# ACT squares q and k, the softmax is issued two heads ahead, and v is split at the turn

## The chip, the cores and the metric

One core of a Trainium2 chip runs the whole program. The metric is the device time of one execution in microseconds (us). TensorE is called PE, VectorE DVE, ScalarE ACT, GpSimd POOL; SP is the queue from which nearly all transfers are issued.

## What is computed

The reference is an attention with a root-mean-square norm on q and k, and two mixers behind it:

```python
batch, n_heads, seq, head_dim = (4, 12, 448, 64)
q_n, k_n = (rmsnorm(q, g_q), rmsnorm(k, g_k))     # x / sqrt(mean(x*x) + 1e-6) * g
scores = scale * np.matmul(q_n, k_n.transpose(0, 1, 3, 2))
scores = scores - np.max(scores, axis=-1, keepdims=True)
attn = np.exp(scores)
attn = attn / (np.sum(attn, axis=-1, keepdims=True) + 1e-09)
out = np.matmul(attn, v)
# mixer 1: u = x + (U V applied over tokens);  y = u + relu(u @ w_ch1) @ w_ch2   (768 -> 3072 -> 768)
# mixer 2: u = x + (w_tok1, relu, w_tok2 over tokens); out = u + relu(u @ w_ch1) @ w_ch2   (768 -> 1536 -> 768)
```

There are 4 x 12 = 48 heads of 448 tokens by 64 values, all in float32.

## The kernel before

The program works in stages. In the first, the **lone stage**, PE has nothing but attention: the 24 heads of the first two batches (12 pairs of heads). Then the mixers of these two batches run, with the attention of the other 24 heads spread among their matmuls; the loop that does this takes one step of `attention` for so many matmul steps of the mixer (`run`). The last stages are mixers alone. `attention` is a generator: one step `t` of it issues one head's product and another head's softmax. The step at which the lone stage ends is called the seam (`seam` = 24).

For a pair of heads the work is this, with its lines:

- `fetch_heads` (L359) loads q, k and v of the pair, 112 partitions by 512 values each. q and k share 5 buffers (tag `qkr`), v has 3.
- `load_pair` squares q and k into `sq` (L373, one buffer), sums the squares on DVE into `ms` (L374), makes 1/sqrt of the mean by Ln and Exp on ACT and a Newton step (L376 to L384), and multiplies it in to give `qn` and `kn` (L392). Squares and these multiplications are one function `mul`: DVE for pairs 0, 2 and 3, POOL for all others. Behind that, still in `load_pair`, v is split into a high and a low part `vs` (L144 on ACT, L145 on POOL), except the even head of a lone-stage pair, which is multiplied whole.
- `turn_pair` transposes `qn` and `kn` on PE (L410), splits them into high and low halves `both` (L417 and L421 on ACT, L418 and L422 on DVE), and sends them through eight transfers on the SP queue into the tiles `qs` and `ks` of the two heads (L433, L434; three buffers each).
- `softmax` makes the scores of a head in four chunks of 112 rows: two matmuls into a bank `sc` (L79; three banks in the lone stage), the row maximum on DVE (`nm`, L451), the exponential with its sum on ACT (`p`, L453), and for each two chunks the reciprocal of the sums (L456, L457) and the scaling of `p` on POOL (L460). `p` has 12 tiles in the lone stage, three heads.
- `weigh` is the product with v: for each of four column blocks PE transposes the four `p` tiles (`pt`, L479), ACT copies the result to `ph` (L490), DVE takes the rest `pl` (L494; for whole heads there is no `pl`, and DVE copies every second `ph`, L488), and PE multiplies them with v into `pv` (L79). The result goes to `xT` by DVE (L499, or ACT's `tmp` L502 and DVE's L503).

In step `t`, softmax of head `t+1` and product of head `t` are issued by turns, then `turn_pair` of the pair of head `t+3`, `fetch_heads` of head `t+7`'s, `load_pair` of head `t+5`'s, where those are even. That is the order in which the program is written. A scheduler then sorts the instructions of each engine within the limits of tiles and banks; the order in which an engine executes is what it decided, and each engine takes its instructions strictly in that order.

Right behind the seam the first weights of the mixer are converted (`to_f32`: load `w_raw` L116, ACT L125 and L130, DVE L126, L127, L131, POOL L134; split L144, L145), and `rank_mix` transposes `xT` (L552) as its first step.

Of the kernel before, what the change touches and what calls it, by code (L numbers as in the profile page):

```python
# [9 lines left out]
F32 = mybir.dt.float32  # L10
# [3 lines left out]
AF = mybir.ActivationFunctionType  # L14
# [10 lines left out]
def attention_then_two_mixers(  # L25
# [30 lines left out]
    nc = tc.nc  # L56
# [43 lines left out]
    pools = {"late": False, "split_u": nc.gpsimd}  # L100
    AT = dict(qr=5, kr=5, vr=3, qn=1, vs=2, p=8, ph=3, pl=3, sq=1)

# [260 lines left out]

    def load_pair(b, hp, whole, turn, qk):
        first = turn == 0
        mul = nc.vector.tensor_mul if turn in (0, 2, 3) else nc.gpsimd.tensor_mul
        qr, kr, vr = qk + fetch_heads(b, hp, "v")

        ms = pools["at"].tile([CP, 2, 8], F32, tag="ms", name="ms")
        for i, t in enumerate((qr, kr)):  # L370
            sq = pools["at"].tile([CP, 2 * NC4, D], F32, tag="sq", bufs=AT["sq"], name="sq")
            tt = t.rearrange("p h c d -> p (h c) d")
            mul(sq, tt, tt)  # L373
            nc.vector.reduce_sum(ms[:, i], sq, axis=AX.X)  # L374
# [4 lines left out]
        nc.scalar.activation(rs, rs, AF.Exp, scale=-0.5)  # L379
        nt = pools["at"].tile([CP, 2, 8], F32, tag="nt", name="nt")  # L380
        small.tensor_mul(nt, rs, rs)
# [12 lines left out]
        qn, kn = qn[0], kn[0]  # L394

        vs = pools["at"].tile([CP, 2, NC4, 2, D], F32R, tag="vs", bufs=AT["vs"], name="vs")
        js = [j for j in range(2) if j not in whole]
# [3 lines left out]
        flat = vr.rearrange("p h c d -> p (h c d)")  # L401
        return qn, kn, [flat[:, j * NC4 * D:] if j in whole else vs[:, j] for j in range(2)]

# [101 lines left out]
    def attention(pairs, seam):  # L505

        n = 2 * len(pairs)
        loaded, turned, probs, fetched = {}, {}, {}, {}  # L510
        dst = None

        def soft(h):
            if not 0 <= h < n:
                return iter(())
            probs[h] = []
            return softmax(probs[h], *turned[h // 2][h % 2])

        for t in range(-7, n):
            if t == seam:  # L520
                for _ in soft(t):
                    pass
            steps = [soft(t + 1) if t + 1 != seam else iter(())]
            if t >= 0:
                if t % 2 == 0:
                    dst = pairs[t // 2][3]()
                steps.append(weigh(
                    probs.pop(t), loaded[t // 2][2][t % 2], t % 2, dst, t % 2 in pairs[t // 2][2]))
# [7 lines left out]
            h = t + 7  # L536
            if h < n and h % 2 == 0:
                fetched[h // 2] = fetch_heads(*pairs[h // 2][:2], "qk")
            h = t + 5
            if 0 <= h < n and h % 2 == 0:  # L540
                loaded[h // 2] = load_pair(
                    *pairs[h // 2][:3], h // 2, fetched.pop(h // 2))
                if h == 0:
                    turned[0] = turn_pair(*loaded[0][:2], first=True)
            yield t

# [491 lines left out]
    with ExitStack() as stack:  # L1038
# [128 lines left out]
```

## Time and profile before

| | us |
|---|---|
| median of 3 runs | 1530.44 (1529.71 to 1535.4) |
| the profiled execution's own time | 1532.7 |
| its span, first to last instruction | 1530.9 |
| PE busy in the span | 1440.5 (94%) |
| DVE busy | 1170.5 (76%) |
| POOL busy | 921.8 (60%) |
| ACT busy | 742.7 (49%) |

The profiled execution is 2.3 us above the median of the runs, and its span 1.8 us below its own time. Busy time of PE is the time in which a matmul is somewhere in its pipeline, so it overstates how full the engine is. These shares are means over all stages; the change touches the attention, and most of it the lone stage, the first 201 us or so.

### The profile page before, as it was taken

What the parts mean: (1) busy time and instruction counts of PE and PEld (TensorE: products, weight loads), DVE (VectorE), ACT (ScalarE), POOL (GpSimd) and SP (SyncE); (2) the same over time, 40 slices, a digit from 0 to 9 for tenths busy, and PEclk for the clock granted to TensorE, in tenths of its full rate; (3) what the DMA queues carried; (4) which work ended last, traced back from release to release, by engine and by line L of the source; (5) the groups of instructions that cost most, each with busy time, mean ns of one, the idle gap of its engine ahead of it and who ended that gap; (6) DMA issues with size and microseconds to landing.
All of it is one profiled execution on the core that took longest, in us unless ns stands there. A gap on an engine that the chain in (4) does not pass through costs nothing.

```text
span 1530.9 us, 22094 instructions
## 1 busy us (share of the span) xinstructions
PE 1440.5 (94%) x7396; PEld 1271.6 (83%) x7396; DVE 1170.5 (76%) x1793; ACT 742.7 (49%) x1508; POOL 921.8 (60%) x955
## 2 busy tenths in 40 slices
PE   4889978999999999999999999998999999999998
PEld 3667656888899889988888998897999998988997
DVE  7888777887877778666757766477888888578876
ACT  4777655656665665444535343335343431334421
POOL 5899857877876655455645454037777755206841
PEclk9999979999999999999999999999999999999999
DMA  6666545867766664765637664354545453424343
GB/s 171 159 163 162 145 162 183 250 193 218 253 220 203 184 208 171 258 227 175 214 128 240 227 231 143 116 194 134 177 127 183 127 186 129 134 85 127 119 122 103
DMA packets 144385, 266.06 MB, mean 174 GB/s; under 512 B 12832, under 2 KB 104448, under 8 KB 144160
## 3 DMA queue, kind: packets, MB, share of 16 engines
q1 hardware_dynamic: 143952, 264.65, 55.5%
q8 instruction: 59, 0.97, 0.3%
q14 instruction: 54, 0.44, 0.1%
q10 hardware_dynamic: 320, 0.00, 0.0%
HBM read 149.72 MB, written 79.10 MB: 149 GB/s over the span
## 4 chain that ended last, share of the span: by engine, by line
PE 63%; DVE 11%; POOL 8%; DMA 7%; ACT 5%; issue 4%; SPq 1%; ACTq 0%; POOLq 0%; DVEq 0%
PE ps_x L79 26%; PE ps_g L79 12%; PE ps_p L79 10%; PE pv L79 3%; PE sc L79 3%; PE pt L479 2%; POOL w_bits L134 2%; PE ps_u L79 2%; POOL w L145 2%; PE ps_t L79 2%; DMA qs<-both 2%; DVE w_bits L126 1%; POOL p L460 1%; DMA w_raw<-in_moe_w_ch_dram 1%; DMA c_a<-w_bits 1%
## 5 line engine op out<-in xcount | busy, mean ns | idle before, releaser
L79 PE MATMUL ps_x<-gs,w 128*128 128x448 f32 x1440 | 323.9, 371 | 9.6 <-DVE xT L668 5.3
L79 PE MATMUL ps_g<-u,w 128*128 128x448 f32 x1440 | 313.1, 370 | 4.3 <-DMA w<-h_a 1.8
L79 PEld LDWEIGHTS ps_x<-gs,w 128*128 128x128 f32 x1440 | 266.7, 189 | 35.4 <-DVE xT L668 8.4
L79 PEld LDWEIGHTS ps_g<-u,w 128*128 128x128 f32 x1440 | 269.4, 189 | 28.8 <-DVE u L565 2.1
L79 PE MATMUL ps_x<-gs,w_b 128*128 128x448 f32 x1026 | 228.8, 369 | 7.1 <-DVE xT L833 2.4
L79 PEld LDWEIGHTS ps_x<-gs,w_b 128*128 128x128 f32 x1026 | 192.9, 189 | 25.9 <-DVE xT L833 3.8
L134 POOL TENSOR_TENSOR w_bits<-w_bits,w_round 128x768 uint32<-128x768 uint32 (+3 forms) x80 | 144.9, 1812 | 109.3 <-DVE w_bits L131 59.5
L145 POOL TENSOR_TENSOR w<-w_bits,w 128x768 fp32r<-128x768 f32 (+3 forms) x82 | 145.4, 1780 | 73.1 <-ACT w L144 69.3
L668 DVE TENSOR_TENSOR xT<-ps_x,xT 128x448 f32<-128x448 f32 x216 | 132.2, 617 | 36.5 <-PE ps_x L79 33.7
L145 POOL TENSOR_TENSOR w_b<-w_f,w_b 128x384 fp32r<-128x384 f32 x104 | 118.3, 1152 | 59.1 <-ACT w_b L144 58.9
L295 POOL TENSOR_TENSOR w_f<-w_f 128x384 f32<-128x384 f32 x26 | 36.2, 1391 | 179.8 <-DMA w_f<-c_b 75.0
L460 POOL TENSOR_SCALAR p<-p,sm 112x448 f32<-112x448 f32 x192 | 133.1, 706 | 17.5 <-DVE sm L457 10.9
L453 ACT ACTIVATE p<-sc,nm 112x448 f32<-112x448 f32 x192 | 121.3, 635 | 45.8 <-DVE nm L451 40.3
L79 PE MATMUL sc<-ks,qs 128*112 128x448 f32 x384 | 120.9, 407 | 15.9 <-ACT p L453 11.3
L451 DVE TENSOR_REDUCE nm<-sc 112x1 f32<-112x448 f32 x192 | 116.2, 614 | 17.6 <-PE sc L79 16.8
L479 PEld LDWEIGHTS pt<-ident,p 112*112 112x112 f32 x768 | 89.8, 134 | 33.2 <-issue 10.4
L126 DVE TENSOR_SCALAR w_bits<-w_bits 128x768 f32<-128x768 f32 (+3 forms) x80 | 71.9, 898 | 56.6 <-ACT w_bits L125 56.5
L479 PE MATMUL pt<-ident,p 112*112 112x112 f32 x768 | 111.9, 261 | 2.5 <-DVE pl L494 0.8
L130 ACT ACTIVATE w_round<-w_raw 128x768 uint32<-128x768 uint32 (+3 forms) x80 | 69.8, 873 | 77.6 <-POOL w_bits L134 69.9
L490 ACT ACTIVATE ph<-pt 112x448 fp32r<-112x448 f32 (+1 forms) x168 | 88.2, 544 | 26.2 <-PE pt L479 25.5
L637 ACT ACTIVATE gs<-ps_g 128x448 fp32r<-128x448 f32 x88 | 47.3, 541 | 108.8 <-PE ps_g L79 107.9
L125 ACT ACTIVATE w_bits<-w_raw 128x768 f32<-128x768 f32 (+3 forms) x80 | 69.8, 874 | 61.7 <-POOL w L145 33.1
(141 smaller groups left out, 2766.2 us busy)
## 6 DMA issues: line engine op xcount, KB each, us to landing
w_raw<-in_moe_w_ch_dram SPq DMA_DIRECT2D x72, 768.0 KB, 5.1
w_b<-h_a SPq DMA_DIRECT2D x65, 384.0 KB, 4.3
h_a<-w SPq DMA_DIRECT2D x56, 384.0 KB, 3.1
ks<-both SPq DMA_DIRECT2D x92, 224.0 KB, 3.8
c_a<-w_bits SPq DMA_DIRECT2D x40, 384.0 KB, 4.7
w_f<-c_a SPq DMA_DIRECT2D x40, 384.0 KB, 3.2
h_b<-w SPq DMA_DIRECT2D x32, 384.0 KB, 2.6
w_b<-h_b SPq DMA_DIRECT2D x29, 384.0 KB, 3.8
```

Of the source, the lines that this page charges most:

```text
L79: nc.tensor.matmul(o, lhsT=l, rhs=r, start=start, stop=stop)
L125: nc.scalar.activation(f(w), f(high), AF.Abs)
L126: nc.vector.tensor_scalar_max(f(w), f(w), TINY)
L130: nc.scalar.activation(r, low, AF.Copy, scale=2.0 ** -29)
L134: nc.gpsimd.tensor_tensor(w, w, r, op=ALU.add)
L145: nc.gpsimd.tensor_sub(lo, w, f(hi))
L451: nc.vector.tensor_reduce(nm, sc, axis=AX.X, op=ALU.max, negate=True)
L453: nc.scalar.activation(p, sc, AF.Exp, bias=nm, accum_out=sm[:, c % 2:c % 2 + 1])
L460: nc.gpsimd.tensor_scalar(x, x, sm[:, i:i + 1], 1.0, op0=ALU.mult, op1=ALU.mult)
L479: nc.tensor.transpose(pt[:, c * CP:(c + 1) * CP], pr[c][:, kc * CP:(kc + 1) * CP], ident[:CP, :CP],)
L490: nc.scalar.activation(ph, pt, AF.Copy)
L668: nc.vector.tensor_add(xT[:, dc], px, xT[:, dc])
```

## The change

```diff
-    AT = dict(qr=5, kr=5, vr=3, qn=1, vs=2, p=8, ph=3, pl=3, sq=1)
+    AT = dict(qr=5, kr=5, vr=3, qn=1, vs=2, p=8, ph=3, pl=3, sq=2)
...
-    def load_pair(b, hp, whole, turn, qk):
+    def load_pair(b, hp, turn, qk):
         first = turn == 0
-        mul = nc.vector.tensor_mul if turn in (0, 2, 3) else nc.gpsimd.tensor_mul
+        mul = nc.vector.tensor_mul if first else nc.gpsimd.tensor_mul
...
         for i, t in enumerate((qr, kr)):
...
-            mul(sq, tt, tt)
+            if turn >= NP * 2:
+                nc.gpsimd.tensor_mul(sq, tt, tt)
+            elif first and i:
+                nc.vector.tensor_mul(sq, tt, tt)
+            else:
+                nc.scalar.activation(sq, tt, AF.Square)
             nc.vector.reduce_sum(ms[:, i], sq, axis=AX.X)
...
+        return qn, kn, vr
+
+    def split_v(vr, whole):
         vs = pools["at"].tile([CP, 2, NC4, 2, D], F32R, tag="vs", bufs=AT["vs"], name="vs")
...
-        for t in range(-7, n):
+        for t in range(-8, n):
+            ahead = 2 if t < seam else 1
             if t == seam:
                 for _ in soft(t):
                     pass
-            steps = [soft(t + 1) if t + 1 != seam else iter(())]
+            steps = [soft(t + ahead) if t >= seam or t + ahead < seam else iter(())]
...
-            h = t + 3
-            if 0 < h < n and h % 2 == 0:
+            def due(steps):
+                h = t + steps
+                if h % 2:
+                    h += 1
+                    return h if h < min(n, seam) else n
+                return h if h < n and h >= seam else n
+
+            h = due(3)
+            if 0 < h < n:
                 turned[h // 2] = turn_pair(*loaded[h // 2][:2], second=h == 2)
+                values[h // 2] = split_v(loaded[h // 2][2], pairs[h // 2][2])
...
-        AT.update(p=8, ph=3, pl=3)
+        AT.update(p=8, ph=3, pl=2)
```

- In the lone stage ACT takes the squares (23 instructions; the k of pair 0 is squared by DVE). The multiplications for `qn` and `kn` of pairs 2 and 3 go from DVE to POOL. `sq` has two buffers. From pair 12 on POOL squares, as before.
- In the lone stage the softmax of head `t+2` is written beside the product of head `t`. Turn, load and fetch of a pair are written one step earlier (`due`), so that they keep their distance to the softmax.
- v is split where the pair is turned, one pair of heads later than before.
- To make room, `ms` and `nt` have one buffer in place of two, and behind the seam `pl` has two in place of three. The lone stage keeps its 12 tiles of `p` and 3 banks of `sc`.

The change moves instructions at three places on which the prediction rests. First PE in mid-stage, where the product of head 8 (the ninth) begins. In the kernel before, `p_1025` is the first tile of head 8, `ks_1122` the keys of head 10:

```order
L479 MATMUL pt_1171<-ident_67,p_1025 112x112
L479 MATMUL pt_1171<-ident_67,p_1042 112x112
L479 MATMUL pt_1171<-ident_67,p_1065 112x112
L479 MATMUL pt_1171<-ident_67,p_1083 112x112
L79 MATMUL sc_1326<-ks_1122,qs_1121 112x448 x2
```

In the changed kernel `p_988` is the first tile of head 8, and `ks_1071` holds the keys of head 10:

```order
L487 MATMUL pt_1206<-ident_67,p_988 112x112
L487 MATMUL pt_1206<-ident_67,p_1003 112x112
L487 MATMUL pt_1206<-ident_67,p_1023 112x112
L487 MATMUL pt_1206<-ident_67,p_1038 112x112
L79 MATMUL sc_1248<-ks_1071,qs_1070 112x448 x2
```

What moved: nothing. In both orders the last chunk of head 10's scores stands behind the first transposes of head 8, so the eleven chunks before it (of heads 8, 9 and 10) have been issued ahead of these transposes. From head 7 on this count is 2.75 heads at 14 of the 15 heads up to head 21 in the kernel before (2.5 at the other), and 2.75 or 3.00 in the changed one; in the first heads it is smaller in the changed kernel (1.50, 1.75, 2.00 and 2.25 for heads 0 to 3, where it was 1.75, 2.25, 2.75 and 2.75).

Second, the start of the program on ACT: `rs` is the factor of pair 0 (two instructions), `vs` the splits of v. In the kernel before:

```order
L378 ACTIVATE rs<-ms 112x16
L379 ACTIVATE rs<-rs 112x16
L144 ACTIVATE vs<-vr 112x4x64 x2
L417 ACTIVATE both<-tt,gg 128x448
L421 ACTIVATE both<-tt 128x448
```

In the changed kernel:

```order
L378 ACTIVATE sq<-qr 112x512 x2
L144 ACTIVATE vs<-vr 112x4x64
L378 ACTIVATE sq<-kr 112x512
L383 ACTIVATE rs<-ms 112x16
L144 ACTIVATE vs<-vr 112x4x64
L384 ACTIVATE rs<-rs 112x16
L378 ACTIVATE sq<-qr 112x512
```

And DVE at the same place. `gg` is the product of the two gains, which come by a transfer; `nt` and `rs` the Newton step of pair 0, `ms` the sums of squares. In the kernel before:

```order
L91 TENSOR_TENSOR gg<-gq_72,gk_73 128x1
L92 TENSOR_SCALAR gg<-gg 128x1
L381 TENSOR_TENSOR nt<-rs 112x16
L382 TENSOR_TENSOR nt<-nt,ms 112x16
L383 TENSOR_SCALAR nt<-nt 112x16
L374 TENSOR_REDUCE ms<-sq 112x8
L384 TENSOR_TENSOR rs<-rs,nt 112x16
L392 TENSOR_TENSOR qn<-qr,rs 112x2x4x64
```

In the changed kernel:

```order
L91 TENSOR_TENSOR gg<-gq_72,gk_73 128x1
L381 TENSOR_SCALAR ms<-ms 112x16
L92 TENSOR_SCALAR gg<-gg 128x1
L386 TENSOR_TENSOR nt<-rs 112x16
L387 TENSOR_TENSOR nt<-nt,ms 112x16
L388 TENSOR_SCALAR nt<-nt 112x16
L379 TENSOR_REDUCE ms<-sq 112x8 x2
L389 TENSOR_TENSOR rs<-rs,nt 112x16
L397 TENSOR_TENSOR qn<-qr,rs 112x2x4x64
L397 TENSOR_TENSOR kn<-kr,rs 112x2x4x64
```

What moved: two squares of pair 1 and both splits of v now stand ahead of the second half of pair 0's factor on ACT, and on DVE both sums of pair 1 ahead of `rs`, where one stood.

Third, POOL in mid-stage, a stretch of about one head in the kernel before:

```order
L460 TENSOR_SCALAR p<-p,sm 112x448 x2
L145 TENSOR_TENSOR vs<-vr,vs 112x4x64
L373 TENSOR_TENSOR sq<-kr 112x512
L382 TENSOR_TENSOR nt<-nt,ms 112x16
L456 TENSOR_SCALAR sm<-sm 112x2
L460 TENSOR_SCALAR p<-p,sm 112x448 x2
L383 TENSOR_SCALAR nt<-nt 112x16
L456 TENSOR_SCALAR sm<-sm 112x2
L384 TENSOR_TENSOR rs<-rs,nt 112x16
L376 TENSOR_SCALAR ms<-ms 112x16
L373 TENSOR_TENSOR sq<-qr 112x512
L392 TENSOR_TENSOR qn<-qr,rs 112x2x4x64
```

In the changed kernel, one head as well:

```order
L397 TENSOR_TENSOR qn<-qr,rs 112x2x4x64
L389 TENSOR_TENSOR rs<-rs,nt 112x16
L468 TENSOR_SCALAR p<-p,sm 112x448 x4
L464 TENSOR_SCALAR sm<-sm 112x2
L145 TENSOR_TENSOR vs<-vr,vs 112x4x64
L468 TENSOR_SCALAR p<-p,sm 112x448 x2
L464 TENSOR_SCALAR sm<-sm 112x2
L468 TENSOR_SCALAR p<-p,sm 112x448 x2
L381 TENSOR_SCALAR ms<-ms 112x16
L397 TENSOR_TENSOR kn<-kr,rs 112x2x4x64
L464 TENSOR_SCALAR sm<-sm 112x2
L386 TENSOR_TENSOR nt<-rs 112x16
```

What moved: the squares are gone from POOL; its scalings of `p` and its normalisations stay.

## Rows read from the trace of the kernel before

**Rows 1.** Busy time by stretch: length, engines' busy us (instructions), PE clock, DMA.

```profile
core 0: us, PE busy (x) PEld busy (x) DVE busy (x) ACT busy (x) POOL busy (x), PEclk, DMA share, GB/s
28.00:60.00 32.00, 27.69 (x143) 20.34 (x142) 26.61 (x56) 22.11 (x63) 26.88 (x53) 0.90 0.72 183
60.00:100.00 40.00, 34.72 (x203) 25.68 (x201) 33.91 (x72) 29.15 (x82) 33.68 (x60) 1.00 0.66 159
100.00:140.00 40.00, 38.32 (x216) 27.70 (x214) 34.98 (x74) 31.97 (x90) 36.84 (x69) 1.00 0.62 153
140.00:180.00 40.00, 37.41 (x215) 27.57 (x216) 33.22 (x71) 30.55 (x85) 34.93 (x68) 1.00 0.65 159
```

**Rows 2.** PE's waits, 28 to 196 us: us in total, times, longest.

```profile
PE sc L79 <- ACT p L453: 5.3, 8, 1.5
PE sc L79 <- DMA ks<-both: 4.3, 4, 1.9
PE pv L79 <- ACT ph L490: 2.0, 5, 0.6
PE pv L79 <- DVE pl L494: 1.6, 4, 0.6
PE tt L410 <- POOL p L460: 0.8, 1, 0.8
```

**Rows 3.** PE in order of time, mid-stage: start, us, instruction, count.

```profile
109.48 1.04 PE L79 MATMUL sc<-ks,qs 128*112 128x448 f32 x4
110.36 0.92 PE L79 MATMUL pv<-ph,vr 112*128 112x448 f32 x2
111.11 0.55 PE L479 MATMUL pt<-ident,p 112*112 112x112 f32 x4
111.49 0.93 PE L79 MATMUL pv<-ph,vr 112*128 112x448 f32 x2
...
118.77 0.36 PE L79 MATMUL pv<-ph,vs 112*128 112x448 f32 x1
118.97 0.55 PE L479 MATMUL pt<-ident,p 112*112 112x112 f32 x4
```

**Rows 4.** Single lines: count, ns (min/median/max), first and last start.

```profile
L373 POOL TENSOR_TENSOR sq<-qr x21: 1035/1040/1755, 6.2 to 423.3; 112x512 f32<-112x512 f32 x21
L373 DVE TENSOR_TENSOR sq<-qr x3: 693/694/991, 3.3 to 16.7; 112x512 f32<-112x512 f32 x3
L392 DVE TENSOR_TENSOR qn<-qr,rs x3: 680/693/1480, 9.7 to 40.4; 112x512 f32<-112x512 f32 x3
L144 ACT ACTIVATE vs<-vr x2: 617/624/631, 187.1 to 198.7; 112x512 fp32r<-112x512 f32 x2
```

**Rows 5.** All engines in order of time, 0 to 20 us.

```profile
7.67 0.16 DVE L91 TENSOR_TENSOR gg<-gq,gk 128x1 f32<-128x1 f32 x1 [1.33 <-DMA qr<-in_q_dram]
...
8.41 0.42 ACT L144 ACTIVATE vs<-vr 112x256 fp32r<-112x256 f32 x1 [1.58 <-DMA vr<-in_v_dram]
...
9.69 1.48 DVE L392 TENSOR_TENSOR qn<-qr,rs 112x512 f32<-112x512 f32 x1
...
9.80 0.42 ACT L144 ACTIVATE vs<-vr 112x256 fp32r<-112x256 f32 x1 [0.97 <-DMA vr<-in_v_dram]
...
11.10 1.21 DVE L392 TENSOR_TENSOR kn<-kr,rs 112x512 f32<-112x512 f32 x1
```

**Rows 6.** All engines in order of time at the seam, 186 to 202 us.

```profile
191.71 0.45 SPq L116 DMA_DIRECT2D w_raw<-in_moe_w_ch_dram  x1
...
197.16 0.89 ACT L125 ACTIVATE w_bits<-w_raw 128x768 f32<-128x768 f32 x1 [2.75 <-DMA w_raw<-in_moe_w_ch_dram]
...
199.27 0.96 DVE L131 SCALAR_TENSOR_TENSOR w_bits<-w_raw,w_bits 128x768 uint32<-128x768 uint32 x1
...
200.26 0.62 DVE L503 TENSOR_TENSOR xT<-pv,tmp 64x448 f32<-64x448 f32 x1
...
201.03 1.19 PE L79 MATMUL ps_h<-xs,w 112*128 112x384 f32 x2 [5.18 <-DVE xT L503]
```

More of the change, by code (lines that the diff above doesn't have):

```diff
@@ L362, in fetch_heads @@
         return res
-    def load_pair(b, hp, whole, turn, qk):
+    def load_pair(b, hp, turn, qk):
         first = turn == 0
-        mul = nc.vector.tensor_mul if turn in (0, 2, 3) else nc.gpsimd.tensor_mul
+        mul = nc.vector.tensor_mul if first else nc.gpsimd.tensor_mul
         qr, kr, vr = qk + fetch_heads(b, hp, "v")
-        ms = pools["at"].tile([CP, 2, 8], F32, tag="ms", name="ms")
+        ms = pools["at"].tile([CP, 2, 8], F32, tag="ms", bufs=1, name="ms")
         for i, t in enumerate((qr, kr)):
@@ L379, in load_pair @@
         nc.scalar.activation(rs, rs, AF.Exp, scale=-0.5)
-        nt = pools["at"].tile([CP, 2, 8], F32, tag="nt", name="nt")
+        nt = pools["at"].tile([CP, 2, 8], F32, tag="nt", bufs=1, name="nt")
         small.tensor_mul(nt, rs, rs)
@@ L401, in load_pair @@
         flat = vr.rearrange("p h c d -> p (h c d)")
-        return qn, kn, [flat[:, j * NC4 * D:] if j in whole else vs[:, j] for j in range(2)]
+        return [flat[:, j * NC4 * D:] if j in whole else vs[:, j] for j in range(2)]
     def turn_pair(qn, kn, first=False, second=False):
@@ L509, in attention @@
         n = 2 * len(pairs)
-        loaded, turned, probs, fetched = {}, {}, {}, {}
+        loaded, turned, values, probs, fetched = {}, {}, {}, {}, {}
         dst = None
@@ L527, in attention @@
                 steps.append(weigh(
-                    probs.pop(t), loaded[t // 2][2][t % 2], t % 2, dst, t % 2 in pairs[t // 2][2]))
+                    probs.pop(t), values[t // 2][t % 2], t % 2, dst, t % 2 in pairs[t // 2][2]))
             for _ in zip_longest(*steps):
@@ L532, in attention @@
                 pairs[t // 2][4](dst)
-            h = t + 3
-            if 0 < h < n and h % 2 == 0:
+            def due(steps):
[6 more added lines that the diff above has]
+            if 0 < h < n:
                 turned[h // 2] = turn_pair(*loaded[h // 2][:2], second=h == 2)
-            h = t + 7
-            if h < n and h % 2 == 0:
+                values[h // 2] = split_v(loaded[h // 2][2], pairs[h // 2][2])
+            h = due(7)
+            if h < n:
                 fetched[h // 2] = fetch_heads(*pairs[h // 2][:2], "qk")
-            h = t + 5
-            if 0 <= h < n and h % 2 == 0:
+            h = due(5)
+            if 0 <= h < n:
                 loaded[h // 2] = load_pair(
-                    *pairs[h // 2][:3], h // 2, fetched.pop(h // 2))
+                    *pairs[h // 2][:2], h // 2, fetched.pop(h // 2))
                 if h == 0:
                     turned[0] = turn_pair(*loaded[0][:2], first=True)
+                    values[0] = split_v(loaded[0][2], pairs[0][2])
             yield t
```

## The prediction

> **What bounds the kernel now.** I read the busy time by stretch first, then PE's waits, then PE in order of time, and last the start and the seam. The lone stage runs from the first instruction to about 201 us, and only there does the change take work from one engine to another. Between 60 and 180 us all four engines are nearly full [rows 1]: in 100 to 140 us PE is busy for 38.32 of 40 us, POOL for 36.84, DVE for 34.98 and ACT for 31.97. A pair of heads needs 72 matmul instructions on PE (16 `sc`, 32 `pt`, 16 `pv`, 8 `tt`); 216 of them in these 40 us are three pairs, so a pair takes 13.33 us.
>
> PE looks full there, but busy is not work. From start to start, four `sc` take 0.88 us, two halves of a `pv` with a whole v 0.75, four transposes 0.38, and one `pv` with a split v 0.20 [rows 3]. That is 16 x 0.22 + 8 x 0.38 + 4 x 0.75 + 8 x 0.20 + 2 x 0.38 = 11.9 us a pair. Some 1.4 us of each pair is waiting, part of it inside the busy time.
>
> What PE visibly waits for [rows 2] is first of all ACT: 5.3 us for a bank of scores that the exponential has to free, 2.0 us for `ph`. Then come the key transfers (4.3 us), DVE's `pl` (1.6 us), and POOL with 0.8 us. POOL is the fullest helper, yet PE hardly waits for it, because scaled tiles lie ready.
>
> **The change, part by part.** *The softmax two heads ahead* costs and gains nothing from head 7 on: the order of PE has scores 2.75 heads ahead of the product in both kernels, since the 12 tiles of `p` were the limit already. I give it no term of its own; what the smaller lead in the first four heads does is part of the start below.
>
> *The start.* `gg` begins at 7.67 us, when its gains land [rows 5], and `qn` of pair 0 at 9.69; `kn` ends at 12.31. In the changed order the second half of pair 0's factor stands on ACT behind the second split of v, which cannot begin before v lands: 9.80 + 0.42 = 10.2 us. Before, the small steps, one sum `ms` and `rs` took about 1.8 us from the end of the gains' two steps to `qn`. Now a second sum stands ahead of `rs` (0.6 us more, about the time of a square on DVE [rows 4]), and ACT's own step is some 0.3 (an estimate): `qn` at about 12.9 us. If POOL leaves the two multiplications alone they take 0.69 us each, as the DVE square of the same shape does, and end at 14.3, +2.0 us; at 1.48 and 1.21 as now, at 15.6, +3.3. It could also cost nothing, if PE is held by something later. I take **+2.0** (0 to +3.3).
>
> *The early heads.* DVE loses five squares and four multiplications of 0.69 us, 6.2 us, all before 42 us [rows 4]. PE is idle for 4.3 us in 28 to 60 us [rows 1], behind transfers whose sources DVE makes. I take half of it back, **-2.0** (0 to -4.3): the other half is the transfers' own time.
>
> *The squares in mid-stage.* From pair 4 on POOL loses two of 1.04 us a pair, ACT gains two. No square on ACT is in this trace; the nearest row is a copy of the same shape on ACT, 0.624 us [rows 4]. So for three pairs in 40 us POOL goes from 36.84 to 30.6 us and ACT from 31.97 to 35.7. PE's visible idle time in 60 to 180 us is 5.28 + 1.68 + 2.59 = 9.55 us. By rows 2, 7.3 of the 14.0 us of waits name ACT, the rest transfers, DVE and POOL. The rest, 48%, is 4.6 us here; POOL's earlier normalisations free the q and k buffers, so the fetches and the transfers queued behind them on SP go sooner. I take two thirds, **-3.0**, and leave the part that names ACT as it is: POOL's answers come sooner to it, but it is fuller. Bounds: -12.6, if all 1.4 us of waiting of nine pairs go; +11.2, if all 18 squares of 0.624 us of these pairs lie on PE's path.
>
> Here the Trainium skill speaks against the change: "ScalarE: Activation LUTs", "Rules for kernel authors", wants multiplications on VectorE, not on ScalarE. In these rows ACT is not the slower one, 0.624 us against 0.694; and by that rule DVE would have 34.98 + 6 x 0.69 = 39.1 of 40 us, and the term would be a loss.
>
> *The split of v* moves, its cost does not. It still waits for the same product to free `vs`, and it stands beside it in ACT's order as before. The v tiles are held longer, which can delay the v transfer on SP; at the seam that matters, next.
>
> *The seam.* PE stands still for 5.18 us [rows 6], because the last `xT` is queued on DVE behind the first weight's conversion, whose transfer was issued at 191.71 and let ACT begin at 197.16. In the changed order `xT` stands ahead of L131 (0.96 us), and ACT makes `tmp` before the split of 0.62 us. So `xT` can begin at 199.3 and not 200.26: **-0.9** (+1 to -5.2; the transfer now follows a v transfer that waits for POOL's split instead of PE's product, and that can go either way).
>
> *Behind the seam* POOL squares as before and the mixers' matmuls fill PE. Two `pl` tiles in place of three could make PE wait. The nearest row is 1.6 us for `pl` in the whole lone stage, with three. I take **0** (-1.6 to +1.6).
>
> **Sum:** +2.0 - 2.0 - 3.0 - 0.9 = -3.9. The profiled execution's own time is 1532.7, so 1528.8 for one like it; that execution lies 2.3 us above the median of the runs, so I forecast **1526.5 us**. A measurement of this kernel can tell about 0.5%, 7.7 us, from no change, so this counts as within.
>
> **Rivals.** *PE comes close to its own work* (faster). If POOL's load is what makes the chain late, the relief is worth more: two thirds of 1.4 us over nine pairs, 8.4, and 0.9 at the seam, with start and early heads cancelling: 1530.4 - 9.3 = 1521. For it: POOL is the fullest helper. Against it: PE names POOL for 0.8 us in all. The Trainium skill's "Perfetto Trace Analysis", "Identifying the Most-Contended Engine", leans to it too: it judges PE by weight loads, 27.70 of 40 us [rows 1], and ranks POOL first.
>
> *ACT becomes the bound* (slower). Scores have three banks, and ACT's exponential frees them. Each square put ahead of an exponential holds PE by its length, 18 x 0.62 = 11.2 us, and the start's 2.0 isn't won back: 1530.4 + 13.2 = 1543.6. It decides once ACT has no idle time left between exponentials. For it: ACT is what PE waits for. Against it: ACT still has 4.3 of 40 us free.
>
> *Nothing moves* (same). The two-heads-ahead issue is already there, PE goes on at 13.33 us a pair, and the ends cancel: 1530. For it: both orders are nearly the same on PE.
>
> **Chances.** Forecast 0.42, nothing 0.26, PE close to its work 0.22, ACT the bound 0.10. A few cases of the forecast pass the limit of 1522.8 us: faster 0.24, same 0.66, slower 0.10. The range of 8 in 10 takes in the better half of the faster rival and the mild cases of ACT holding PE (half of the slower rival's cost): 1518 to 1536.
>
> **What would show it.** Right: `qn` of pair 0 later by about 2 us; POOL near 31, ACT near 36 of 40 us in mid-stage; a pair in about 13.0 us; PE's wait at the seam near 4 us; ACT still first among PE's waits. Wrong: a pair in under 12.6 or over 13.6 us; a pause of PE at the seam that grows; waits of ACT's squares for fetches, with PE behind them; a changed time in the mixers.

## The result and the profile after

| | before | changed |
|---|---|---|
| median of the runs, us | 1530.44 (5 runs, 1526.85 to 1535.4 and one of 7658.42) | 1545.86 (5 runs, 1543.51 to 1552.2) |
| ratio, 95% interval | | 1.0118 [1.0095, 1.0141] |
| last `xT` of the lone stage begins, us (two profiles each) | 200.26, 198.17 | 211.49, 210.05 |
| span less that time, us (two profiles each) | 1330.6, 1330.7 | 1338.7, 1338.3 |

The change makes the kernel slower by 1.2%. 1526.5 was predicted, with a range up to 1536. The two lower rows divide one profiled execution at the seam, and they repeat within 2.1 us and 0.4 us for the same kernel. So in the profiles the lone stage ends 11.6 us later and what follows takes 7.8 us more, 19.4 together. Both profiled executions of the changed kernel are longer than its median (1551.98 and 1550.2 us), so how the 15.4 us between the medians are shared between the two parts is not shown.

Busy time by stretch in the changed kernel, with the columns of [rows 1]:

```profile
28.00:60.00 32.00, 25.69 (x143) 17.99 (x142) 26.15 (x54) 26.07 (x73) 22.29 (x50) 1.00 0.79 195
60.00:100.00 40.00, 35.34 (x204) 25.71 (x201) 31.84 (x67) 30.37 (x82) 29.34 (x63) 1.00 0.62 150
100.00:140.00 40.00, 33.52 (x190) 24.68 (x191) 32.82 (x69) 32.10 (x89) 30.36 (x57) 1.00 0.61 138
140.00:180.00 40.00, 33.90 (x175) 24.79 (x174) 28.30 (x60) 26.11 (x70) 30.03 (x57) 0.89 0.57 137
```

Between 100 and 180 us PE now does 365 matmul instructions where [rows 1] had 431. At 72 a pair that is 15.8 us a pair against 13.4. From 28 to 100 us nothing is lost: 347 against 346. And no engine has become full. ACT does more per pair, 11.5 us against 10.4 (58.21 us over 5.07 pairs, 62.52 over 5.99), and still is busy less of the time than before. Everyone waits, and the question is for whom.

PE's waits from 28 to 196 us, which answer to [rows 2]:

```profile
PE sc L79 <- ACT p L461: 16.2, 15, 3.1
PE pv L79 <- ACT ph L498: 4.7, 4, 2.9
PE sc L79 <- DMA ks<-both: 1.1, 1, 1.1
PE tt L418 <- DVE both L426: 0.6, 1, 0.6
PE tt L418 <- POOL qn L397: 0.6, 1, 0.6
```

The wait for ACT's exponential has tripled, from 5.3 to 16.2 us. What ACT was doing instead is in its groups of instructions, 28 to 190 us (after the bar: busy time and mean ns, then the idle time just before the group and what ended it). First the split of q into `qq` in the kernel before, then the same group and the two of the squares in the changed one:

```profile
L417 ACT ACTIVATE both<-tt,gg 128x448 fp32r<-128x448 f32 x12 | 7.6, 635 | 10.4 <-DMA qs<-both 5.3 <-PE sc L79 2.4 <-issue 1.3
```

```profile
L425 ACT ACTIVATE both<-tt,gg 128x448 fp32r<-128x448 f32 x11 | 7.0, 634 | 20.5 <-DMA qs<-both 14.7 <-DMA qr<-in_q_dram 2.9 <-issue 2.8
L378 ACT ACTIVATE sq<-kr 112x512 f32<-112x512 f32 x9 | 5.7, 634 | 0.5 <-DMA kr<-in_k_dram 0.4
L378 ACT ACTIVATE sq<-qr 112x512 f32<-112x512 f32 x8 | 5.1, 632 | 1.0 <-DMA qr<-in_q_dram 0.9
```

The squares cost what was assumed, 0.63 us each, and hardly wait. The split of q waits: 20.5 us in 11 instructions, 14.7 of them for `qs`, the transfers that read the one `qq` tile for the pair before. Here is one such place, ACT in order of time:

```profile
128.60 0.54 ACT L498 ACTIVATE ph<-pt 112x448 f32<-112x448 f32 x1
131.02 0.63 ACT L425 ACTIVATE both<-tt,gg 128x448 fp32r<-128x448 f32 x1 [1.87 <-DMA qs<-both]
131.55 0.63 ACT L461 ACTIVATE p<-sc,nm 112x448 f32<-112x448 f32 x1
132.06 0.20 ACT L461 ACTIVATION_READ_ACCUMULATOR p<-sc,nm 112x1 f32 x1
132.16 0.63 ACT L461 ACTIVATE p<-sc,nm 112x448 f32<-112x448 f32 x1
```

The SP queue shortly before (issues):

```profile
125.30 0.87 SPq L442 DMA_DIRECT2D qs<-both  x1
126.22 1.00 SPq L441 DMA_DIRECT2D ks<-both  x1
127.26 0.59 SPq L442 DMA_DIRECT2D qs<-both  x1
```

And PE:

```profile
130.49 0.93 PE L487 MATMUL pt<-ident,p 112*112 112x112 f32 x8
132.32 0.66 PE L79 MATMUL sc<-ks,qs 128*112 128x448 f32 x2 [0.90 <-ACT p L461]
```

ACT is done with `ph` at 129.14 us. The next instruction in its order is the split of the next pair's q, and the last transfer out of `qq` was only issued at 127.26. So ACT stands still until 131.02, with three exponentials behind the split, and PE stands 0.90 us for a score bank that the first of them frees. Those transfers were late themselves, because SP waits for scores to free a `qs` tile (7.0 us at a stretch between 117 and 129 us). That wait, 28 to 190 us, in the kernel before and in the changed one:

```profile
SPq L434 <- PE sc L79: 26.6, 12, 4.6
```

```profile
SPq L442 <- PE sc L79: 43.5, 11, 8.4
```

The pairs are ready to be turned earlier than their target tiles come free. For pair 9 (the tenth), the multiplication that makes its `qn` on POOL, and the split of its q on ACT, in the kernel before:

```profile
123.44 1.04 POOL L392 TENSOR_TENSOR qn<-qr,rs 112x512 f32<-112x512 f32 x1
127.59 0.65 ACT L417 ACTIVATE both<-tt,gg 128x448 fp32r<-128x448 f32 x1
```

In the changed kernel its split is the one at 131.02 us above, and its `qn` is this:

```profile
107.73 1.04 POOL L397 TENSOR_TENSOR qn<-qr,rs 112x512 f32<-112x512 f32 x1
```

`qn` begins 15.7 us sooner and the split 3.4 us later. What POOL gained has become waiting.

### The profile page after: what moved, and what is told of

It is laid out like the page before. It is cut to its first block, busy times and chain, and to the rows that moved or that the text cites. A ratio compares the mean times of both kernels' runs of the same rounds, so it can differ in the third digit from the quotient of the medians.

```text
span 1550.2 us, 22122 instructions
## 1 busy us (share of the span) xinstructions
PE 1444.7 (93%) x7396; PEld 1274.2 (82%) x7396; DVE 1164.7 (75%) x1784; ACT 755.7 (49%) x1531; POOL 910.1 (59%) x941
## 4 chain that ended last, share of the span: by engine, by line
PE 57%; DMA 11%; DVE 11%; POOL 8%; ACT 7%; issue 4%; SPq 2%; ACTq 0%; POOLq 0%; DVEq 0%
PE ps_x L79 24%; PE ps_p L79 10%; PE ps_g L79 10%; DMA qs<-both 4%; PE sc L79 3%; PE pv L79 2%; POOL w_bits L134 2%; DMA w_raw<-in_moe_w_ch_dram 2%; DVE w_bits L131 2%; POOL w L145 2%; DVE w_bits L126 2%; PE ps_u L79 2%; PE pt L487 2%; PE ps_t L79 2%; ACT p L461 2%
## 5 line engine op out<-in xcount | busy, mean ns | idle before, releaser
L79 PE MATMUL sc<-ks,qs 128*112 128x448 f32 x384 | 124.1, 415 | 32.0 <-ACT p L461 27.9
L468 POOL TENSOR_SCALAR p<-p,sm 112x448 f32<-112x448 f32 x192 | 136.5, 723 | 25.5 <-DVE sm L465 19.1
L459 DVE TENSOR_REDUCE nm<-sc 112x1 f32<-112x448 f32 x192 | 116.0, 612 | 26.5 <-PE sc L79 25.7
L79 PEld LDWEIGHTS sc<-ks,qs 128*112 128x112 f32 x384 | 62.6, 186 | 51.6 <-ACT p L461 40.2
```

The lines of the kernel that those rows point to most:

```text
L79: nc.tensor.matmul(o, lhsT=l, rhs=r, start=start, stop=stop)
L459: nc.vector.tensor_reduce(nm, sc, axis=AX.X, op=ALU.max, negate=True)
L468: nc.gpsimd.tensor_scalar(x, x, sm[:, i:i + 1], 1.0, op0=ALU.mult, op1=ALU.mult)
```

## The experiments

Sixteen kernels and a second profile of each of the two. The table has the last `xT` of the lone stage, what the split of `qq` waited for `qs` transfers between 28 and 190 us, the span less that `xT`, the median, and its ratio to the runs of before that were made beside it (these have medians of 1528.2 to 1529.5 us).

| kernel | last `xT` | split for `qs` | rest of span | median us | ratio [95%] |
|---|---|---|---|---|---|
| before_again | 198.2 | 2.8 | 1330.7 | 1528.85 | 0.9997 [0.9977, 1.0018] |
| after_again | 210.1 | 13.8 | 1338.3 | 1547.11 | 1.0119 [1.0074, 1.0164] |
| squares_alone | 206.8 | 19.0 | 1333.0 | 1544.96 | 1.0107 [1.0069, 1.0146] |
| order_alone | 195.0 | 2.4 | 1334.7 | 1531.5 | 1.0032 [1.0009, 1.0056] |
| neither | 193.3 | 1.7 | 1340.3 | 1534.15 | 1.0024 [1.0001, 1.0048] |
| two_qq | 199.7 | 0 | 1336.0 | 1536.12 | 1.0052 [1.0029, 1.0075] |
| four_qk | 203.7 | 4.5 | 1340.6 | 1545.85 | 1.0096 [1.0069, 1.0123] |
| no_squares | 198.8 | 15.6 | 1331.3 | 1533.68 | 1.0021 [1.0001, 1.0040] |
| squares_twice | 196.3 | 6.1 | 1335.7 | 1535.74 | 1.0041 [1.0019, 1.0063] |
| late_squares_two_qq | 197.2 | 0 | 1349.1 | 1547.77 | 1.0107 [1.0080, 1.0134] |
| pl_three | 204.6 | 11.4 | 1334.4 | 1539.76 | 1.0073 [1.0054, 1.0092] |
| two_qq_pl_three | 200.4 | 0 | 1341.3 | 1538.65 | 1.0051 [1.0027, 1.0075] |
| neither_pl_three | 192.9 | 1.0 | 1339.4 | 1536.64 | 1.0061 [1.0030, 1.0092] |
| before_two_qq | 192.4 | 1.8 | 1338.1 | 1531.51 | 1.0017 [0.9994, 1.0040] |
| before_pl_two | 198.4 | 3.1 | 1339.0 | 1536.71 | 1.0053 [1.0032, 1.0074] |
| order_two_qq | 192.9 | 0 | 1336.1 | 1531.17 | 1.0014 [0.9997, 1.0032] |
| split_alone | 198.1 | 3.4 | 1335.2 | 1535.07 | 1.0047 [1.0028, 1.0065] |
| split_two_qq | 193.4 | 2.0 | 1330.6 | 1525.86 | 0.9985 [0.9970, 1.0000] |

### Which part of the change loses the time

`squares_alone` undoes the earlier order:

```diff
-            ahead = 2 if t < seam else 1
+            ahead = 1
...
             def due(steps):
                 h = t + steps
-                if h % 2:
-                    h += 1
-                    return h if h < min(n, seam) else n
-                return h if h < n and h >= seam else n
+                return h if h % 2 == 0 else n
```

> The changed kernel with the softmax one head ahead and the turn, the loads and the fetches written where they stood before; the squares stay on ACT. Theory L (ACT's load and the order that comes with the squares make it late): the loss stays whole, 1541 to 1548 us, and ACT's split of qq waits some 8 us or more for the qs transfers between 100 and 190 us. Theory T (the turn written one head earlier and the softmax two heads ahead put the split of qq in front of exponentials too soon): 1528 to 1534 us, with those waits near the 2.4 us of before.

`order_alone` undoes the squares instead (and `sq` has one tile again):

```diff
-        mul = nc.vector.tensor_mul if first else nc.gpsimd.tensor_mul
+        mul = nc.vector.tensor_mul if turn in (0, 2, 3) else nc.gpsimd.tensor_mul
...
-            if turn >= NP * 2:
-                nc.gpsimd.tensor_mul(sq, tt, tt)
-            elif first and i:
-                nc.vector.tensor_mul(sq, tt, tt)
-            else:
-                nc.scalar.activation(sq, tt, AF.Square)
+            mul(sq, tt, tt)
```

> The changed kernel with the squares back on POOL and DVE, with one sq tile, and the two multiplications of pairs 2 and 3 back on DVE; two heads ahead, the earlier turn and the later split of v stay. Theory L: 1527 to 1534 us. Theory T: 1540 to 1548 us, with PE waiting for p some 10 us between 100 and 190 us, as in the changed kernel.

`neither` has both of these edits.

> The changed kernel with both of these undone: what is left is the split of v at the turn, one ms, one nt and two pl tiles behind the seam. Theories L and T both: within 3 us of before, 1528 to 1534 us. If the split of v or the pl tiles are the cause (theory V): 1540 us or more; with pl alone at fault the loss lies behind 212 us and the last xT of the lone stage comes at 200 us as before.

The squares alone bring the loss, 1.0107 against 1.0118, and ACT's wait at the split with it; the order alone brings 1531.5 us and hardly any such wait. In the lone stage the squares cost 206.8 - 193.3 = 13.5 us, the order 1.7, and both together 17.5 (210.8, the mean of two profiles, against 193.3). These 13.5 us belong to the whole edit: to the squares of all pairs, the second `sq` tile, and the multiplications of pairs 2 and 3 that went to POOL with them. The split's group in `squares_alone`, then in `order_alone`:

```profile
L425 ACT ACTIVATE both<-tt,gg 128x448 fp32r<-128x448 f32 x12 | 7.6, 634 | 20.1 <-DMA qs<-both 19.0 <-issue 1.2
```

```profile
L420 ACT ACTIVATE both<-tt,gg 128x448 fp32r<-128x448 f32 x12 | 7.6, 636 | 12.3 <-issue 6.3 <-PE tt L413 2.5 <-DMA qs<-both 2.4
```

`neither` missed its range by a little (1534.15 us, up to 1534 expected): its lone stage is 5.9 us shorter than that of before (the mean of two, 199.2), and it is slower all the same, because the rest takes 9.6 us more. Both facts are taken up below.

### Whether the split's wait is the way in which it is lost

`two_qq` gives odd pairs a `qq` of their own:

```diff
-            both = pools["at"].tile([P, 2, S], F32R, tag="qq" if scale else "kk",
+            both = pools["pp" if alt and scale else "at"].tile([P, 2, S], F32R, tag="qq" if scale else "kk",
...
-                turned[h // 2] = turn_pair(*loaded[h // 2][:2], second=h == 2)
+                turned[h // 2] = turn_pair(*loaded[h // 2][:2], second=h == 2,
+                                           alt=h < seam and h // 2 % 2 == 1)
```

> The changed kernel with a second tile for the split of q (qq): pairs with an odd number take theirs from the lone stage's own pool, so that ACT's split no longer waits for the qs transfers of the pair before. If the wait of that split, with exponentials queued behind it, is how the time is lost: the mid-stage gets 8 to 11 us back, 1533 to 1538 us, and PE's wait for p falls from 11.1 to under 4 us. If ACT's mere busy time is what holds PE: within 3 us of the changed kernel, 1542 to 1549 us.

The wait is gone and PE's for `p` falls from 11.1 to 3.9 us between 100 and 190 us. The lone stage ends 11.1 us earlier, the median falls by 9.7. The split's group now reads:

```profile
L425 ACT ACTIVATE both<-tt,gg 128x448 fp32r<-128x448 f32 x11 | 7.2, 654 | 0.5 <-issue 0.5
```

The second tile has the program sorted anew in the lone stage, and that alone can be worth several us there: `pl_three` below, which there only takes its second `sq` tile from another pool, ends the lone stage 6.2 us before the changed kernel. But of the kernels with the squares on ACT, the three with a second `qq` end it at 197.2 to 200.4 us, the four without (the changed kernel among them) at 203.7 to 210.8.

`four_qk` leaves the single `qq` and gives every fourth head its own `qs` and `ks` (`alt` as in `two_qq`):

```diff
-            qs = pools["at"].tile([P, S], F32R, tag="qs", bufs=3, name="qs")
-            ks = pools["at"].tile([P, 2, S], F32R, tag="ks", bufs=3, name="ks")
+            own = pools["pp"] if alt and j else pools["at"]
+            bufs = 1 if alt and j else 3
+            qs = own.tile([P, S], F32R, tag="qs", bufs=bufs, name="qs")
+            ks = own.tile([P, 2, S], F32R, tag="ks", bufs=bufs, name="ks")
```

> The changed kernel with a fourth tile each of qs and ks: the second head of pairs with an odd number takes its own from the lone stage's pool; qq stays single. In the changed kernel SP waited 35.8 us between 100 and 190 us for scores to free a qs tile. If that wait is what brings the qs transfers late, and with them ACT's split of the next qq: SP's wait falls under 20 us, the split's wait for qs from 14.7 us (28 to 190 us) to under 6, and the time to 1533 to 1540 us. If the transfers' own 3.2 us and SP's queue are enough to keep the single qq taken: SP's wait falls and the split's stays over 10 us, 1541 to 1548 us.

Both waits fall as the first theory has it: SP's for scores from 43.5 to 12.5 us (28 to 190 us), the split's from 14.7 to 4.5. The lone stage ends 7.1 us earlier than in the changed kernel. But ACT's squares of k now wait 7.7 us for their fetch, where they waited 0.5, and the rest of the span takes 2.1 us more than in the changed kernel, so the time came out as the second theory had it. As a test of the total it is a miss; for the lone stage it agrees with `two_qq`.

### ACT's load or POOL's relief

The squares do two things at once: they load ACT and relieve POOL. Each was done without the other. `no_squares` relieves POOL alone. It leaves out the squares of pairs 4 to 11, so its result is not the attention. Order and start are as before; the edit is shown against `neither`:

```diff
+            tt = t.rearrange("p h c d -> p (h c) d")
+            if 4 <= turn < NP * 2:
+                nc.vector.tensor_reduce(ms[:, i], tt, axis=AX.X, op=ALU.max)
+                continue
             sq = pools["at"].tile([CP, 2 * NC4, D], F32, tag="sq", bufs=AT["sq"], name="sq")
-            tt = t.rearrange("p h c d -> p (h c) d")
             mul(sq, tt, tt)
             nc.vector.reduce_sum(ms[:, i], sq, axis=AX.X)
```

> The order of writing and the start as before, with the squares of pairs 4 to 11 left out: DVE takes the largest element of each row of q and k in place of the sum of squares, in an operation of the same shape, so POOL is relieved as by the change and ACT is given nothing. Theory E (relieving POOL alone makes the turns come early, into a single qq that is still being read): the split of qq waits for qs for 8 us or more between 28 and 190 us, and the time is 1533 to 1541 us, no better than before. Theory L (what ACT is given is what holds it): under 4 us of those waits and 1522 to 1530 us.

`squares_twice` loads ACT alone, again against `neither`:

```diff
             mul(sq, tt, tt)
             nc.vector.reduce_sum(ms[:, i], sq, axis=AX.X)
+            if 4 <= turn < NP * 2:
+                sq = pools["at"].tile([CP, 2 * NC4, D], F32, tag="sa", bufs=1, name="sa")
+                nc.scalar.activation(sq, tt, AF.Square)
```

> The order of writing and the start as before, squares on POOL as before, and ACT squares the q and k of pairs 4 to 11 a second time into a tile of its own that nothing reads: ACT is loaded as by the change, POOL is not relieved. Theory L: 1541 to 1548 us, PE waiting for p some 10 us between 100 and 190 us. Theory E: 1531 to 1539 us, within a few us of the kernel with neither part (1534), and the split of qq waits for qs for less than 4 us between 28 and 190 us.

The split's group, in `no_squares`, then in `squares_twice`:

```profile
L423 ACT ACTIVATE both<-tt,gg 128x448 fp32r<-128x448 f32 x12 | 7.6, 635 | 16.5 <-DMA qs<-both 15.6 <-issue 0.6 <-PE tt L416 0.3
```

```profile
L423 ACT ACTIVATE both<-tt,gg 128x448 fp32r<-128x448 f32 x12 | 7.6, 636 | 8.2 <-DMA qs<-both 6.1 <-PE tt L416 1.3 <-PE sc L79 0.7
```

So it is POOL's relief that brings the wait: 15.6 us of it without a single square on ACT, and 6.1 with all of those of pairs 4 to 11 there (more than the 4 that theory E allowed). `qn` and `kn` come early and the split cannot follow: from the start of pair 9's `qn` to the start of its split it is 4.1 us in the kernel before and in `neither` and 5.2 in `squares_twice`, but 23.3 in the changed kernel, 18.4 in `squares_alone` and 18.8 in `no_squares`. Against `neither` the relief alone makes the lone stage 5.5 us longer and the load alone 3.0, where the squares as they are cost 13.5. Neither of the smaller two is above what a new order alone can make there. The stage says more when it is cut at the `xT` of the 4th, 11th, 19th and 24th head (us; two profiles where there are two):

| kernel | to the 4th | 4th to 11th | 11th to 19th | 19th to 24th |
|---|---|---|---|---|
| before | 67.6, 67.0 | 47.8, 47.3 | 54.4, 53.2 | 30.5, 30.6 |
| changed | 67.5, 68.8 | 53.7, 52.6 | 62.7, 62.1 | 27.7, 26.5 |
| `neither` | 62.6 | 49.9 | 51.4 | 29.4 |
| `squares_alone` | 67.3 | 50.2 | 57.1 | 32.2 |
| `no_squares` | 64.7 | 48.9 | 57.7 | 27.5 |
| `squares_twice` | 65.8 | 50.0 | 50.0 | 30.6 |
| `two_qq` | 71.0 | 49.3 | 53.3 | 26.1 |

ACT's last square in the changed kernel begins at 118.6 us (in `squares_alone` at 116.3), before the 11th `xT`; the squares are taken far ahead, and from pair 12 on POOL squares again:

```profile
L378 ACT ACTIVATE sq<-kr x11: 613/631/645, 8.8 to 118.6; 112x512 f32<-112x512 f32 x11
```

The 11th and the 19th `xT` in `squares_alone`, then in `no_squares`:

```profile
117.60 0.60 DVE L507 COPY xT<-pv 64x448 f32<-64x448 f32 x1
174.66 0.61 DVE L507 COPY xT<-pv 64x448 f32<-64x448 f32 x1
```

```profile
113.67 0.60 DVE L505 COPY xT<-pv 64x448 f32<-64x448 f32 x1
171.35 0.60 DVE L505 COPY xT<-pv 64x448 f32<-64x448 f32 x1
```

From the 11th to the 19th head ACT has no square in either, and both take some 6 us more than `neither`; `squares_twice`, with two squares left there, takes no more than it. Between the 4th and the 11th, with 7 squares on ACT in `squares_alone`, 5 in `squares_twice` and none in the other two, these four kernels are within 1.3 us of each other. So what is lost in the middle comes with POOL's relief and the wait at the split, whether ACT has squares or not; no price of ACT's load is seen there. Ahead of the 4th `xT`, where most of the other squares lie, `squares_alone` loses 4.8 us against `neither`, `squares_twice` 3.2, and `no_squares`, which has none, 2.1. How much of that is ACT's load and how much the new order is not shown.

### Behind the seam

`pl_three` takes the second `sq` tile from the lone stage's pool and returns the third `pl`:

```diff
-            sq = pools["at"].tile([CP, 2 * NC4, D], F32, tag="sq", bufs=AT["sq"], name="sq")
+            own = pools["pp" if i and turn < NP * 2 else "at"]
+            sq = own.tile([CP, 2 * NC4, D], F32, tag="sq", bufs=1, name="sq")
...
-        AT.update(p=8, ph=3, pl=2)
+        AT.update(p=8, ph=3, pl=3)
```

> The changed kernel with three pl tiles and one sq tile behind the seam, as before the change; the second sq tile of the lone stage comes from the stage's own pool. The order behind the seam is made anew by this. If the two pl tiles cost time behind the seam (theory P): the lone stage as slow as in the changed kernel, 8 to 10 us behind before at its end, but 1536 to 1541 us in all. If nothing is lost by two pl tiles: 1542 to 1549 us.

`two_qq_pl_three` has this and the second `qq` tile.

> The same with the second qq tile. The kernel with two qq ended the lone stage level with before and 5.7 us later in all (1536.1 against 1530.4). Theory P: 1527 to 1533 us. Without it: 1533 to 1540 us.

`neither_pl_three` is `neither` with the last line of that diff.

> The kernel with neither the squares nor the earlier order (the split of v at the turn, one ms and one nt are left of the change), with three pl tiles behind the seam. With two, its profile was 6.7 us ahead of before at the 900th matmul and 4.7 us behind near the end. Theory P: the lead of the lone stage is kept, 1522 to 1528 us. Without it: 1531 to 1537 us.

`before_pl_two` is the kernel before with `pl=2` in that line.

> The kernel before with two pl tiles behind the seam in place of three and nothing else: the order is the same on PE up to the 1168th instruction, long behind the seam, and made anew after it. Theory P (the loss behind the seam comes with fewer pl tiles and the order they bring): 4 to 11 us slower than before, 1533 to 1540 us, the lone stage unchanged. If the loss behind the seam is the later start of a slow lone stage alone: within 3 us of before.

`late_squares_two_qq` was made for another question, the start:

```diff
-            if turn >= NP * 2:
-                nc.gpsimd.tensor_mul(sq, tt, tt)
-            elif first and i:
-                nc.vector.tensor_mul(sq, tt, tt)
-            else:
+            if 4 <= turn < NP * 2:
                 nc.scalar.activation(sq, tt, AF.Square)
+            else:
+                mul(sq, tt, tt)
```

> The changed kernel with the second qq tile, with the squares of pairs 0 to 3 where they were before (DVE for pairs 0, 2 and 3, POOL for pair 1) and ACT's from pair 4 on. The kernel with two qq lost 2.8 us against before by the 100th matmul and was level again at the end of the lone stage. If the early squares on ACT are what costs at the start: level at the 100th matmul and 1525 to 1532 us in all. If it is the later split of v and the earlier turn: still 2 to 3 us late there and 1533 to 1538 us.

`before_pl_two` leaves the lone stage alone, and the rest of the span grows by 8.3 us. But the number of `pl` tiles is not a cause by itself. With three, the rest takes 1334.4 where the changed kernel has 1338.5; 1339.4 where `neither` has 1340.3; and 1341.3 where `two_qq` has 1336.0. (`pl_three` came into theory P's range, but its lone stage is 5.4 us behind before and not the 8 to 10 of the text; the other two with three tiles did not.) DVE's `pl` waits for ACT's `ph` behind the seam, not for a tile that PE holds. What all of these kernels share is an order on PE between the 900th and the 3,000th matmul that is not that of the kernel before: in the traces 875 to 1,482 of the 2,100 places there hold another instruction (by its tiles), and hardly any behind them (20 at most). An edit of the lone stage alone is enough for that (`before_two_qq`). But the order is not all: the changed kernel, `squares_alone` and `two_qq` have one and the same order on PE from the 900th matmul on, and their rests are 1338.5, 1333.0 and 1336.0. So 2.3 to 7.8 us go with that order, and 5.5 us come and go without a change of it. The rest of the span lies between 1330.6 and 1349.1 us over these kernels, and the kernel before is at the low end of it. `late_squares_two_qq` shows how much the rest can differ: its lone stage ends 2.0 us before that of the kernel before, and its rest takes 18.4 us more, so the kernel is at 1547.77, outside both ranges of its expectation. (On its own question: at the start it stands close to before, 42.4 us at the 100th matmul where before has 42.9 and `two_qq` 44.1, but the total could not tell.) `before_two_qq` is the mildest case: nothing behind the seam is edited, and 7.5 us are lost there. Which instructions lose it was not followed up.

### Second profiles, and what gains

> The kernel before, unchanged, for a second profile of it. The kernels without squares on ACT stood 6 to 7 us ahead of the first profile of before at the 900th matmul. If that first profile is typical: the last xT of the lone stage at 199 to 202 us again. If it was a late one: at 193 to 196 us, and the loss of the changed kernel in the lone stage is then larger by as much.

> The changed kernel, unchanged, for a second profile of it; its runs lie at 1544 and at 1552 us, and the one profiled was of the later ones. If the two differ in the lone stage: the last xT at 203 to 206 us where it was at 211.5. If they differ behind the seam: at 210 to 212 us again, and the time between 467 and 512 us is lost only in the later ones.

The two kernels keep their difference, 199.2 and 210.8 us (means) for the lone stage. The question about 467 to 512 us stays open.

`before_two_qq` is the kernel before with the edit of `two_qq`.

> The kernel before with a second qq tile for odd pairs in the lone stage and nothing else. In the kernel before ACT's split of qq waited 5.3 us for qs transfers between 28 and 190 us, and PE 5.3 us for p. If the price of that wait is about one half of its length, as the runs with and without it suggest: 1526 to 1530 us. If the second tile gains only where ACT also has the squares: 1529 to 1533 us.

`order_two_qq` is `order_alone` with it.

> The changed kernel with the squares where they were before and a second qq tile for odd pairs: two heads ahead, the earlier turn and the split of v at the turn, with the single qq no longer in the way. If the order of the change has a gain of its own that the single qq hid: 1522 to 1527 us, under both kernels. If the mid-stage is at PE's own work without the squares: 1529 to 1536 us.

`split_alone` is the kernel before with `split_v` called where the pair is turned and nothing else, `split_two_qq` the same with the second `qq`.

> The kernel before with one part of the change alone: v is split where the pair is turned. The kernels with neither the squares nor the earlier order, which have this part, ended the lone stage at 193 us, before at 198 to 200. If the later split is what gains there: last xT at 192 to 195 us, and in all 1524 to 1529 us if the order behind the seam comes out as good as before, 1529 to 1537 if it comes out like that of the other kernels (5 to 10 us worse). If the gain came with the smaller ms and nt: last xT at 197 to 200 us.

> The same with a second qq tile for odd pairs in the lone stage. If later split and second tile add up: last xT at 188 to 191 us, 1520 to 1526 us with an order behind the seam as good as before, 1526 to 1534 us with one like the others'. If PE's own work is the limit by then: last xT at 191 to 194 us, as with either alone.

The second tile shortens the lone stage without any square on ACT too: by 6.8 us on before (199.2 to 192.4), by 4.7 on `split_alone`, by 2.1 on `order_alone`. The totals of `before_two_qq` and `order_two_qq` came out in the ranges of no gain all the same, since the rest grew. The later split of v gains nothing there (198.1). Its gain in `neither` came with the smaller `ms` and `nt`: `neither_pl_three` differs from `split_alone` in these two alone and ends the lone stage 5.2 us earlier. That a tile less should help is most likely the order made from it; this is argued, not shown, and which place in that order does it was not followed up. `split_two_qq` has the shorter lone stage and a rest as short as that of before, and is the one kernel under both: 1525.86 us, ratio 0.9985, with an interval that just reaches 1. Its rest was luck, not design: `before_two_qq` has as short a lone stage and 1338.1.

## Why the prediction was wrong, point by point

**What bounds the kernel.** Right as far as it went: ACT's exponentials are first among PE's waits, before and after, and POOL is hardly named. What was left out is the single `qq` tile, which the trace before already showed with 5.3 us of idle time at ACT's split, a row I had not drawn on.

**The squares in mid-stage** is the step that failed: -3.0, bounds -12.6 to +11.2. Measured are 2.4 us more a pair from 100 us on, and +13.5 in the lone stage for the squares alone, of which 8.7 come behind the 4th `xT`. The size of a square was right (0.634 us where 0.624 was taken), and POOL's load (30.36 us in 100 to 140 us where 30.6 was expected, though over 2.64 pairs). ACT's was not: 32.10 us there and not 35.7. Of the 18 squares counted for 60 to 180 us only 9 begin in that stretch. The sentence that failed is that POOL's earlier normalisations let the fetches and transfers behind them go sooner. They are ready sooner (`qn` of pair 9 by 15.7 us) and then wait for `qs` tiles, 43.5 us against 26.6, and what is late next is ACT's split of the next pair (14.7 us of waiting against 5.3), with the exponentials behind it. The prediction asked who waits for PE and who frees buffers, but did not follow the earlier `qn` to the one tile without a second.

Neither of the two rules that it weighed is borne out by the rows. The Trainium skill's "ScalarE: Activation LUTs", "Rules for kernel authors", would keep the multiplications off ScalarE. It was right on the sign, but not by the cost: ACT's square is the cheaper one, 0.634 us against DVE's 0.694 [rows 4], and no loss by ACT's load is seen behind the 4th `xT`. The Trainium skill's "Perfetto Trace Analysis", "Identifying the Most-Contended Engine", put POOL first. Relieving POOL alone gained nothing: 198.8 us at the last `xT` where `neither` had 193.3.

**Two heads ahead** at 0: `order_alone` against `neither` is +1.7 us in the lone stage with single profiles, and 1531.5 against 1534.15 in all (by the ratios 1.0032 against 1.0024, so the totals do not tell). Right within what can be told without the squares; with them the order adds 4.0 us (206.8 to 210.8).

**The split of v** at 0: right, 198.1 against 199.2 in the lone stage.

**The start** at +2.0 (0 to 3.3). `qn` and `kn` of pair 0 in the changed kernel, which answer to [rows 5]:

```profile
13.18 0.72 DVE L397 TENSOR_TENSOR qn<-qr,rs 112x512 f32<-112x512 f32 x1
13.82 0.68 DVE L397 TENSOR_TENSOR kn<-kr,rs 112x512 f32<-112x512 f32 x1
```

`kn` ends at 14.50 where it ended at 12.31, +2.2. Less of it stays: by 28 us PE has begun 34 matmuls where it had 40, and by 100 us it is still six behind, which is about 1 us. **The early heads** at -2.0: nothing of it shows. From 28 to 60 us PE does 143 matmul instructions in both, and its idle time there is 6.3 us, where it was 4.3 [rows 1]. (The granted clock there was 1.00, and 0.90 before, so the idle time alone is no measure of the loss.)

**The seam** at -0.9: about right, and small. PE's pause in the changed kernel, for [rows 6]:

```profile
212.54 0.69 PE L79 MATMUL ps_h<-xs,w 112*128 112x384 f32 x1 [4.69 <-ACT xs L576]
```

4.69 us against 5.18, where a pause near 4 was expected.

**Behind the seam** at 0 (-1.6 to +1.6): measured +7.8, and +2.3 to +5.3 in two kernels of the same order on PE. This term failed too. The prediction looked for a wait of `pl` and found none, rightly. It didn't reckon with the order being sorted anew; the listing of the order would have shown that, and what it is worth could not be read from one trace. Which wait it is that grows stays open.

**The rivals.** "ACT becomes the bound" gave 1543.6, close to 1545.86, and had a chance of 0.10. That is luck: its mechanism was not the one. It wanted ACT without idle time and each square on PE's path. ACT has more idle time than before, and where most is lost, behind the 11th `xT`, it has no squares any more. Of the signs named beforehand, a pair in over 13.6 us came true (15.8) and a changed time in the mixers did; waits of the squares for fetches did not (1.5 us from 28 to 190 us).

## What to carry to other kernels

Before an engine is relieved, follow its product to the next tile that has no second one, and look which engine, in its fixed order, has to wait there and what is queued behind it. Test this by doing the relief without the load and the load without the relief, and compare stretch by stretch, not only at the end. Where a scheduler sorts the whole program, measure each stage by a mark at its end, and take a kernel with an edit that should do nothing as the scale for the rest: here such edits were worth 8 us behind the seam, and 5 to 6 us in the lone stage.

## What was not expected of the hardware

PE's granted clock fell in the lone stage after pauses. From 60 to 200 us, in the kernel before, then in the changed one:

```profile
60.00:200.00 140.00, 124.39 (x707) 90.04 (x705) 115.62 (x238) 102.31 (x277) 119.95 (x223) 0.99 0.62 153
```

```profile
60.00:200.00 140.00, 121.84 (x676) 89.64 (x673) 110.03 (x229) 101.66 (x275) 105.09 (x206) 0.96 0.60 143
```

0.96 is 5.6 us of full-speed time in 140, 0.99 is 1.4, so up to 4.2 of the 11.6 us lost in the lone stage may be the clock's, where PE had work (0.95 and 7.0 us in the second profile). One such stretch lies behind a pause of 2.33 us, in PE's order of time:

```profile
146.98 0.66 PE L79 MATMUL sc<-ks,qs 128*112 128x448 f32 x2 [2.33 <-ACT p L461]
...
148.88 1.70 PE L79 MATMUL pv<-ph,vr 112*128 112x448 f32 x2
```

```profile
148.00:156.00 8.00, 7.82 (x41) 5.94 (x40) 7.57 (x17) 5.52 (x18) 5.25 (x10) 0.81 0.61 153
```

The two matmuls of a whole product, 0.92 us together in [rows 3], took 1.70 there, and the granted clock of the 8 us from 148 us on is 0.81: PE ran for a part of them at the lower of its two levels, 1.2 GHz. `two_qq` had a granted clock of 1.00 from 100 to 180 us, where the changed kernel had 1.00 and then 0.89 in the two halves; how much of its gain is the clock's is not told apart.
